# A two-layer decode kernel: some V tiles as the moving operand, and a new order of its instructions

## The chip, the core and the metric

The kernel runs on one core of one Trainium2 chip. Its time is the device time of that core in microseconds. Five engines work side by side and meet through semaphores: PE (TensorE, matmul; its weight loads are shown as PEld), DVE (VectorE), ACT (ScalarE), POOL (GpSimd) and SP (SyncE), which here only issues DMAs. 16 DMA engines carry all transfers of the core.

## The reference

One token for each of four batches goes through attention on a cache, a gated linear unit, and both again with the same weights:

```python
def _A_ref(x, k_cache, v_cache, wq, wo):          # x: 4 x 1 x 512
    q = (x @ wq).reshape(B, Sq, 32, 128).transpose(0, 2, 1, 3)
    k = jnp.repeat(k_cache, 4, axis=1)            # caches: 4 x 8 x 4096 x 128
    v = jnp.repeat(v_cache, 4, axis=1)
    p = _softmax(jnp.einsum("bhqd,bhkd->bhqk", q, k) * 128 ** -0.5)
    o = jnp.einsum("bhqk,bhkd->bhqd", p, v)
    return o.transpose(0, 2, 1, 3).reshape(B, Sq, 4096) @ wo
def _B_ref(x, w_gate, w_up, w_down):              # 512 -> 1792 -> 512
    h = _sigmoid(x @ w_gate) * (x @ w_up)
    return h @ w_down
x = A_x
x = x + _A_ref(_layernorm(x), A_k_cache, A_v_cache, A_wq, A_wo)
x = x + _B_ref(_layernorm(x), B_w_gate, B_w_up, B_w_down)
x = x + _A_ref(_layernorm(x), A_k_cache, A_v_cache, A_wq, A_wo)
x = x + _B_ref(_layernorm(x), B_w_gate, B_w_up, B_w_down)
```

Everything is bf16. One batch's K is 8 groups x 4096 x 128, 8 MiB, and so is its V; each group serves four query heads.

## The kernel before

**The data.** K and V come as half tiles of 512 KiB (128 partitions x 2048 elements), 16 for the K of a batch and 16 for its V, into a ring of 22 slots in SBUF. Weights have buffers of their own: wq and wo in four pieces of 1 MiB, wg, wu and wd of 1.75 MiB. K of a batch is used by both layers: most of its half tiles stay in their slots from the first layer's scores to the second layer's; the list `again` (L389) names those that are given up and loaded again instead (0, 3, 3 and 1 for the four batches). V is loaded once for each layer.

**The load order.** The string `order` (L388) is the order of all loads in SP's queue: `k` two K half tiles, `V` one group's V for the first layer (two half tiles), `v` one group's V for the second layer, `r` a batch's reloads, digits and other letters the weights. Each load waits for the last reader of its slot, and SP works in order, so a load that waits holds those behind it.

**The work of one batch b.** `attend` (L779) does scores and softmax for 16 heads (`s` = 0 or 1): DVE transposes the K half tiles in place (L537), PE multiplies (`scores`, L540, result S_ps, 16 rows in each of four strips of 32 partitions), DVE finds the maximum (L567 to L586), ACT takes the exponent (L591), PE and ACT turn the probabilities over (PT_ps, L596 to L610) into `pt_sb`. POOL and PE form the denominators. `values` (L635) multiplies with V: V is the stationary operand, 16 matmuls of 4 columns for each half tile, summed in O_ps; DVE scales (L653). `y_proj` (L657) multiplies with wo into Y_ps. `cross` (L698) then does the residual, the norm, gate and up (`glu`, L670), tanh (for the sigmoid), down (L685), residual and norm. `q_proj` (L496) makes the second layer's queries of that batch, `q_spread` (L511) lays them out (perm matmuls, then qbd), and the second layer's attention runs on the K that is still in the ring. Second-layer V work of batch b - 1 is placed between (`use_later`, L827). The last GLU is done for all four batches at once (`last_cross`, L715).

**What sets the order.** The code states operations with an engine, an estimated duration, a priority and the tiles read and written (`_Sched.put`, L46). `place` (L85) plays them through: each engine takes, of the operations that are ready, the one of best priority, SP goes in order, and a load gets the slot that is free first. The result is a fixed instruction order on every engine and a fixed slot for every load; `emit` (L187) writes it out with semaphores. Durations in the code steer that order and nothing else. Dependencies are by key: who writes a key waits for its readers.

Of the kernel before, what the change touches and what calls it, by code (L numbers as in the profile page):

```python
# [15 lines left out]
RAMP = 0.3  # L16

# [20 lines left out]
class _Sched:  # L38
# [7 lines left out]
    def put(self, eng, fns, dur, prio, reads=(), writes=(), dma=None, tiles=(), uses=(), nbytes=0, rate=RATE):  # L46
        op = _Op()
        op.eng, op.dur, op.prio, op.bytes, op.rate = eng, dur, prio, nbytes, rate
        op.fns = list(fns) if isinstance(fns, (list, tuple)) else [fns]
        op.sem, op.inc, op.needed = dma or eng, 16 if dma else 1, dma is not None  # L50
# [34 lines left out]
    def place(self):  # L85
# [17 lines left out]
        ramp = 0  # L103

# [17 lines left out]
        while True:  # L122
# [47 lines left out]
            else:  # L170
                pending[o.eng].remove(o)
                free_at[o.eng] = t + o.dur
# [30 lines left out]
def bass_interleave_layers__gqa_block_cached__glu_gated_glu__decode_kernel(nc, A_x, A_k, A_v, A_wq, A_wo, B_x, B_wg, B_wu, B_wd, out):  # L203
# [18 lines left out]
    NQB = 4  # L222
# [21 lines left out]
    x16 = sb("x16", [P, P], bf)  # L244
# [5 lines left out]
    gs = sb("gs", [P, NF * B])  # L250
    us_sb = sb("us_sb", [P, NF * B])
    hT = sb("hT", [P, NF * B], bf)
# [15 lines left out]
    p_sb = sb("p_sb", [P, 8, P], bf)  # L268
    pt1 = p_sb[:].rearrange("p c x -> p (c x)")[:, 0:512].rearrange("p (c g a h) -> p c g a h", c=8, g=4, a=4)
    NPT = 5  # L270
    pt_sb = [sb(f"pt_sb{i}", [P, 4, 8, 4, R], bf) for i in range(NPT)]
    oT1 = sb("oT1", [P, H], bf)
    oT2 = sb("oT2", [P, H, B], bf)
# [4 lines left out]
    negb = sb("negb", [P, P], bf)  # L278
# [3 lines left out]
    mt = sb("mt", [P, 32])  # L282
# [5 lines left out]
    sel_den = sb("sel_den", [P, 16])  # L288

# [4 lines left out]
    G_ps = ps("G_ps", [P, 512])  # L294
# [17 lines left out]
    S.put("sp", lambda e: e.dma_start(x16[0:16, :], A_x.rearrange("b o (k p) -> (b o k) p", k=KD)), 0.55, 0, writes=["x16"], dma="x")  # L312
# [8 lines left out]
    for key, ap, v in (("negb", negb[:], -1.0 / D), ("mhalf", mhalf, -0.5), ("xT", xT[:], 1.0)):  # L321
        S.put("dve", lambda e, ap=ap, v=v: e.memset(ap, v), 0.08, 0, writes=[key])
# [8 lines left out]
    for name, t, v in (("ml0", ml, 1.0), ("mt", mt, 0.0), ("S0", S_ps[0], 0.0), ("S1", S_ps[1], 0.0), ("S2", S_ps[2], 0.0)):  # L331
        S.put("dve", lambda e, t=t, v=v: e.memset(t[:], v), 0.4, 0, writes=[name])
# [5 lines left out]
    again = ((), ((6, 1), (7, 0), (7, 1)), ((5, 1), (6, 1), (7, 1)), ((7, 1),))  # L338
# [49 lines left out]
    order = '1k0kkkk23VkkVVkVVbdgacVVVuwrvkkkkkkVvkkVVVVVVVvkvvvvkrvkkkkkvvVkVVVVVVVvkvvvvrkkkkkVvvkvkVVVVVVVvvvvvvvvrvvvvvv'  # L388
    again = ((), ((6, 1), (7, 0), (7, 1)), ((5, 1), (6, 1), (7, 1)), ((7, 1),))  # L389
# [27 lines left out]
    def stat(c, n, prio, reads):  # L417
# [7 lines left out]
        fns = [mm(G_ps[:, c:c + n], negb[:], hi, True, False), mm(G_ps[:, c:c + n], negb[:], lo, False, True)]  # L425
        S.put("pe", fns, 0.1, prio, reads=["xs_hi", "xs_lo", "negb"], writes=["G"])
# [11 lines left out]
    def first_norm(prio):  # L438
        S.put("dve", lambda e: e.tensor_reduce(xsum[:, 0:B], x0[:], AX.X, ALU.add), 0.2, prio, reads=["x0"], writes=["xsum0"])
        stat(0, B, prio, ["xsum0"])  # L440
        S.put("dve", lambda e: e.tensor_copy(nm[0], G_ps[:, 0:B]), 0.15, prio, reads=["G"], writes=["nm0"])
# [7 lines left out]
        stat(4, B, prio, ["xsum4"])  # L449
        power(float(DH), G_ps[:, 4:4 + B], "G", rs_q[0], "rs_q0", B, prio)  # L450

    def add_y(b, y, scal, skey, res, rkey, mi, prio):
# [12 lines left out]
            "act", lambda e: e.activation(  # L465
                xw[:, 0, :], xj[:, b, :], ACTF.Square, bias=nm[mi][:, b:b + 1], accum_out=xsum[:, 1:2]
            ), 0.4, prio, reads=["xj", f"nm{mi}"], writes=["xw", "xsum4"],
        )

    def norm(b, mi, mult, rs, rs_key, prio):  # L470

        stat(0, 2, prio, ["xsum0", "xsum4"])
        new, old = nm[1 - mi][:, b:b + 1], nm[mi][:, b:b + 1]
        S.put("dve", lambda e: e.tensor_copy(new, G_ps[:, 0:1]), 0.15, prio, reads=["G"], writes=[f"nm{1 - mi}"])
# [6 lines left out]
                out=dd[:, 1:2], in0=dd[:, 0:1], scalar=dd[:, 0:1], in1=G_ps[:, 1:2], op0=ALU.mult, op1=ALU.add,  # L481
            ), 0.17, prio, reads=["dd", "G"], writes=["dd"],
# [79 lines left out]
    def softmax(u, rs, rs_key, prio):  # L562
# [69 lines left out]
        )  # L632
        return pi

    def values(l, b, s, pi, prio, gis=range(4)):  # L635
        if not len(gis):
            return
        for gi in gis:
# [263 lines left out]
```

## Time and profile before

| what | value |
|---|---|
| time, median of 8 runs | 336.48 us (334.58 to 340.37) |
| profiled execution: time / span | 338.83 us / 337.0 us |
| mean granted PE clock | 0.678 |
| PE busy | 204.5 us (61%), 5184 matmuls |
| DVE busy | 154.3 us (46%) |
| ACT busy | 60.6 us (18%) |
| POOL busy | 27.1 us (8%) |
| SP loads of K, V half tiles | 71, 128 |
| queue of all loads (q1) | 118.24 MB, its packets took 91.8% of 16 engines' span |

The span is from the first to the last instruction of one profiled execution; the time of that execution has a little more around it. The page also draws the span in 40 equal slices. Here are those of PE and DVE in tenths busy, and the PE clock that was granted, in tenths of full speed:

```profile
PE   0244543254486478666756686748627777696885
DVE  4592641002378862054889520417986501224213
PEclk9999999999997555555755555555757555557555
```

No engine is full over the span. The costliest groups of instructions (line, engine, operation, output<-inputs, count, busy us, mean ns of one, idle before them and what ended it):

```profile
L537 DVE STREAM_TRANSPOSE ring<-ring 128x1024 int32<-128x1024 int32 x71 | 85.9, 1228 | 22.7 <-DMA ring<-in_A_k_cache_dram 22.3
L644 PE MATMUL O_ps<-pt_sb,ring 128*128 128x4 bf16 x2048 | 67.2, 166 | 44.6 <-DMA ring<-in_A_v_cache_dram 30.5
L550 PE MATMUL S_ps<-ring,qbd 128*16 128x512 bf16 x512 | 56.6, 587 | 11.4 <-DVE ring L537 9.1
```

Matmuls overlap, so the mean of one is longer than the distance from one to the next.

### The profile page before, as it was taken

Reading aid. Unit: us, or ns where it says so; the run is one execution under the profiler, and the core shown is the slowest. Engines: PE = TensorE matmul, PEld = TensorE weight load, DVE = VectorE, ACT = ScalarE, POOL = GpSimd, SP = SyncE. Lnnn points to the kernel's source line nnn. Section 1 sums busy time; section 2 is a strip of 40 time slices with the busy share of each in tenths; the row PEclk is TensorE's granted clock in tenths of the full one; section 3 lists DMA queues with packets and bytes.
Section 4 is the critical chain, followed back from the end, with each engine's and each line's share of the span. In section 5 each row is a group of like instructions: output and inputs, shape, how many; then the busy total and the mean of one; then the engine's idle time right before and its main releaser. Section 6 shows DMA issues by size and latency. Waiting matters only on the chain.

```text
span 337.0 us, 11572 instructions
## 1 busy us (share of the span) xinstructions
PE 204.5 (61%) x5184; PEld 149.4 (44%) x5184; DVE 154.3 (46%) x390; ACT 60.6 (18%) x152; POOL 27.1 (8%) x106
## 2 busy tenths in 40 slices
PE   0244543254486478666756686748627777696885
PEld 0213222254443238666323466645214467663774
DVE  4592641002378862054889520417986501224213
ACT  1103103000006413000063130000524120002400
POOL 5101001000001101000011110000111010001101
PEclk9999999999997555555755555555757555557555
DMA  6999999999729999999999999988999999879930
GB/s 215 405 399 404 408 391 379 369 406 372 281 65 372 413 410 406 408 407 344 387 369 410 409 407 408 409 322 246 390 411 408 409 372 415 313 255 386 391 146 2
DMA packets 37906, 118.98 MB, mean 353 GB/s; under 512 B 3425, under 2 KB 9313, under 8 KB 37857
## 3 DMA queue, kind: packets, MB, share of 16 engines
q1 hardware_dynamic: 37824, 118.24, 91.8%
q8 instruction: 40, 0.66, 0.8%
q14 instruction: 10, 0.07, 0.1%
q10 hardware_dynamic: 32, 0.00, 0.0%
HBM read 118.23 MB, written 0.00 MB: 351 GB/s over the span
## 4 chain that ended last, share of the span: by engine, by line
DMA 40%; PE 25%; SPq 16%; issue 12%; DVE 5%; ACT 1%; POOLq 0%; POOL 0%; DVEq 0%; ACTq 0%
DMA ring<-in_A_v_cache_dram 25%; DMA ring<-in_A_k_cache_dram 9%; SPq L344 9%; PE O_ps L644 7%; SPq L365 7%; DMA wd<-in_B_w_down_dram 6%; PE S_ps L550 6%; PE Y_ps L304 6%; PE M_ps L304 4%; DVE ring L537 2%; PE G_ps L304 1%; DVE ml L567 1%; PE PT_ps L304 1%; ACT p_sb L591 1%; POOLq L864 0%
## 5 line engine op out<-in xcount | busy, mean ns | idle before, releaser
L537 DVE STREAM_TRANSPOSE ring<-ring 128x1024 int32<-128x1024 int32 x71 | 85.9, 1228 | 22.7 <-DMA ring<-in_A_k_cache_dram 22.3
L644 PE MATMUL O_ps<-pt_sb,ring 128*128 128x4 bf16 x2048 | 67.2, 166 | 44.6 <-DMA ring<-in_A_v_cache_dram 30.5
L644 PEld LDWEIGHTS O_ps<-pt_sb,ring 128*128 128x128 bf16 x2048 | 61.0, 104 | 57.9 <-DMA ring<-in_A_v_cache_dram 36.1
L550 PE MATMUL S_ps<-ring,qbd 128*16 128x512 bf16 x512 | 56.6, 587 | 11.4 <-DVE ring L537 9.1
L591 ACT ACTIVATE p_sb<-S_ps,cols 128x512 bf16<-128x512 f32 x32 | 24.6, 773 | 83.7 <-DVE cols L586 53.4
L653 DVE TENSOR_TENSOR oT<-O_ps,winv 128x12 bf16<-128x12 f32 (+3 forms) x29 | 5.0, 171 | 70.9 <-PE O_ps L644 70.7
L567 DVE TENSOR_REDUCE ml<-S_ps 128x1 f32<-128x512 f32 x32 | 21.5, 673 | 19.8 <-PE S_ps L550 19.8
L304 PE MATMUL Y_ps<-oT,wo 128*128 128x1 bf16 (+1 forms) x640 | 20.5, 166 | 12.8 <-DMA wo<-in_A_wo_dram 7.7
L550 PEld LDWEIGHTS S_ps<-ring,qbd 128*16 128x16 bf16 x512 | 12.9, 108 | 32.9 <-issue 18.5
L304 PEld LDWEIGHTS Y_ps<-oT,wo 128*128 128x128 bf16 x640 | 18.8, 104 | 15.0 <-DMA wo<-in_A_wo_dram 7.8
L304 PE MATMUL PT_ps<-ident_b,p_sb 128*128 128x64 bf16 x128 | 11.3, 230 | 19.3 <-ACT p_sb L591 19.3
L304 PEld LDWEIGHTS PT_ps<-ident_b,p_sb 128*128 128x128 bf16 x128 | 7.2, 116 | 26.4 <-ACT p_sb L591 21.9
L304 PE MATMUL M_ps<-xT,wq 128*128 128x1 bf16 (+1 forms) x512 | 15.4, 165 | 5.2 <-issue 3.7
L304 PEld LDWEIGHTS M_ps<-xT,wq 128*128 128x128 bf16 x512 | 14.6, 104 | 5.7 <-issue 4.0
L615 POOL TENSOR_TENSOR cols<-cols 128x1 f32<-128x1 f32 x16 | 3.1, 193 | 170.1 <-ACT p_sb L591 170.1
L434 POOL TENSOR_TENSOR cols<-cols 128x1 f32<-128x1 f32 (+1 forms) x10 | 6.6, 656 | 123.7 <-DVE cols L430 86.3
L526 ACT ACTIVATE qbd<-M_ps,mask_a 128x64 bf16<-128x64 f32 x32 | 10.0, 313 | 29.2 <-PE M_ps L304 28.5
L465 ACT ACTIVATE xw<-xj,cols 128x4 f32<-128x4 f32 x8 | 2.4, 298 | 70.6 <-DVE xj L460 70.6
L304 PE MATMUL Y_ps<-hT,wd 128*128 128x1 bf16 (+1 forms) x280 | 8.5, 166 | 10.2 <-issue 5.1
L599 ACT ACTIVATE p_sb<-PT_ps 128x512 bf16<-128x512 f32 x16 | 9.6, 597 | 21.7 <-PE PT_ps L304 17.2
L610 ACT ACTIVATE pt_sb<-PT_ps 128x512 bf16<-128x512 f32 x16 | 9.5, 596 | 19.4 <-PE PT_ps L304 19.3
L304 PEld LDWEIGHTS Y_ps<-hT,wd 128*128 128x128 bf16 x280 | 8.0, 104 | 10.6 <-issue 8.9
(103 smaller groups left out, 152.2 us busy)
## 6 DMA issues: line engine op xcount, KB each, us to landing
ring<-in_A_v_cache_dram SPq DMA_DIRECT2D x128, 512.0 KB, 9.6
ring<-in_A_k_cache_dram SPq DMA_DIRECT2D x71, 512.0 KB, 9.6
wq<-in_A_wq_dram SPq DMA_DIRECT2D x4, 1024.0 KB, 14.1
wo<-in_A_wo_dram SPq DMA_DIRECT2D x4, 1024.0 KB, 14.1
wg<-in_B_w_gate_dram SPq DMA_DIRECT2D x1, 1792.0 KB, 13.9
wu<-in_B_w_up_dram SPq DMA_DIRECT2D x1, 1792.0 KB, 16.0
wd<-in_B_w_down_dram SPq DMA_DIRECT2D x1, 1792.0 KB, 20.6
x<-in_A_x_dram SPq DMA_DIRECT2D x1, 4.0 KB, 1.6
```

The lines of the kernel that those rows point to most:

```text
L304: return lambda e: e.matmul(o, lhsT=l, rhs=r, start=start, stop=stop)
L344: return e.dma_start(ring[t.slot], t.src.rearrange("(p t) d -> p (t d)", p=P)[:, q * TS:(q + 1) * TS])
L365: S.put("sp", lambda e: e.dma_start(o, i), 0.43, 0, writes=[key], dma=key, nbytes=nbytes, rate=rate)
L434: "pool", lambda e: e.tensor_tensor(rs, vpe[:, 0:nb], mhalf[:, 0:nb], ALU.pow), 0.6, prio,
L526: "act", lambda e, a=a: e.activation(qbd[u % NQB][:].rearrange("p g n x -> p (g n) x")[:, :, 4 * a:4 * a + 4], M_ps[:, 256:320].rearrange( ...
L537: return e.transpose(v, v)
L550: return e.matmul(bank[32 * gi:32 * gi + 16, :], lhsT=qbd[u % NQB][:, gi, nn, :], rhs=kt[:, :, nn // 2, :, nn % 2], start=nn == 0, stop=nn ...
L567: "dve", lambda e, q=q: e.tensor_reduce(ml[:, q:q + 1], S_ps[banks[q]][:], AX.X, ALU.max, negate=True), 0.65,
L591: "act", lambda e, q=q: e.activation(p_sb[:, 4 * q:4 * q + 4, :].rearrange("p c x -> p (c x)"), S_ps[banks[q]][:], ACTF.Exp, bias=nbias, s ...
L599: "act", lambda e: e.activation(pt1.rearrange("p c g a h -> p (c g a h)"), PT_ps[:], ACTF.Copy), 0.65, prio,
L610: "act", lambda e: e.activation(pt_sb[pi][:].rearrange("p q c g h -> p (q c g h)"), PT_ps[:], ACTF.Copy), 0.65,
L644: return e.matmul(O_ps[:, gi * R:(gi + 1) * R], lhsT=ring[tile.slot][:, (t % HT) * DH:(t % HT + 1) * DH], rhs=pt_sb[pi][:, t % 4, t // 4, ...
```

## The change

- **Wide V.** Second-layer V of batch b - 1 that is used around `cross(b)` for b = 1, 2, 3 (36 half tiles, `NARROW[3]` is empty) goes through the new function `wide`: the probabilities are stationary (8 columns: two key blocks of four heads), V is moving with 256 columns, and the 8 matmuls of a half tile go round four strips of the new bank W_ps. Two groups share the bank's two halves. Then ACT copies W_ps to `w_hi` (bf16), DVE takes the rest into `w_lo`, and four small matmuls a group with the 0/1 matrix `sel_o` sum strips and halves into O_ps. All other V stays as it was.
- **Banks and buffers.** G_ps is gone; gate goes to M_ps, the norms' sums to M_ps or PT_ps. Some buffers are laid over others to make room: gs, us and hT in the second half of p_sb (and they share its key), x16 in w_hi, oT2 on q1T, mt on ml, negb as one column. qbd has 3 buffers, not 4. `pt_sb` has another layout.
- **Small operations.** The sum of squares in `add_y` is on DVE instead of ACT. Gate and up are planned piece by piece, so that they may alternate, and the norm may start after the second of four gate pieces. V and wo of the first layer alternate by group.
- **The planner.** PE durations come from a count of instructions (0.0268 a pair and 0.13 at the end), and at each 256th PE instruction the planner adds a wait if less than 5.7 has passed since the last such point. The priorities, `order` and `again` are new: reloads are 1, 3, 2 and 4 half tiles. The second query spread of the next batch is stated after the first half's attention.

The core of the diff:

```diff
+BLOCK = 256
+FETCH = 5.7
+PAIR = 0.0268
+DRAIN = 0.13
...
+                if o.eng == "pe":
+                    n = 2 * len(o.fns)
+                    to = BLOCK - begun % BLOCK
+                    if n >= to:
+                        at = t + o.dur * to / n
+                        wait = max(0.0, crossed + FETCH - at)
+                        o.dur += wait
+                        crossed = at + wait
+                    begun += n
+                free_at[o.eng] = t + o.dur - (DRAIN if o.eng == "pe" else 0.0)
...
-    NQB = 4
+    NQB = 3
+    WIDE = 0.43
+    NARROW = ((0, 1, 2, 3), (0, 1, 2, 3), (0, 1, 2, 3), (), (0, 1, 2, 3))
...
-    order = '1k0kkkk23VkkVVkVVbdgacVVVuwrvkkkkkkVvkkVVVVVVVvkvvvvkrvkkkkkvvVkVVVVVVVvkvvvvrkkkkkVvvkvkVVVVVVVvvvvvvvvrvvvvvv'
-    again = ((), ((6, 1), (7, 0), (7, 1)), ((5, 1), (6, 1), (7, 1)), ((7, 1),))
+    order = 'k10bkkkkk3Vk2VVkdVVcVagVVuwrvkkkkkkVvkkVVVVVVVvvkvvvkrkkkkvkvvVkVVVVVVVvvkvvvrkkkvvkvkkkVVVVVVVVrvvvvvvvvvvvvvv'
+    again = (((3, 1),), ((6, 1), (7, 0), (7, 1)), ((6, 1), (7, 1)), ((6, 0), (6, 1), (7, 0), (7, 1)))
...
-    PS0, PS1, PL0, PL1, PV0, PV1, PK0, PK1, PDEN, PEV = (1.24, 0.52, 0.5, 1, 1.15, 0.9, 2.1, 2.1, 0.72, 1.8)
+    PS0, PS1, PL0, PL1, PV0, PV1, PK0, PK1, PDEN, PEV = (1.77, 1.93, -0.4, 1.55, 2.05, 1.65, 2.13, 2.82, 2.29, 1.1)
...
+    def wide(l, b, s, pi, prio, gis):
+        n = len(gis)
+        for i, gi in enumerate(gis):
+            for q in range(2):
+                tile = V[l, b, 4 * s + gi, q]
+                fns = []
+                for j in range(HT // 2):
+                    def fn(e, i=i, gi=gi, q=q, j=j, tile=tile):
+                        a, t = j % 4, q * HT + 2 * j
+                        return e.matmul(
+                            W_ps[32 * a:32 * a + 2 * R, i * 256:i * 256 + 256],
+                            lhsT=pt_sb[pi][:, t // 4, gi, t % 4:t % 4 + 2, :].rearrange("p t h -> p (t h)"),
+                            rhs=ring[tile.slot][:, 2 * j * DH:(2 * j + 2) * DH],
+                            start=q == 0 and j < 4, stop=q == 1 and j >= 4,
+                        )
+                    fns.append(fn)
+                S.put("pe", fns, WIDE + DRAIN, prio, reads=[f"pt{pi}"], writes=["W"], tiles=[tile])
+        w = 256 * n
+        S.put(
+            "act", lambda e: e.activation(w_hi[:, 0:w], W_ps[:, 0:w], ACTF.Copy), 0.62 if n > 1 else 0.4, PEV, reads=["W"],
+            writes=["w_hi"],
+        )
+        S.put(
+            "dve", lambda e: e.tensor_tensor(w_lo[:, 0:w], W_ps[:, 0:w], w_hi[:, 0:w], ALU.subtract),
+            0.65 if n > 1 else 0.4, PEV, reads=["W", "w_hi"], writes=["w_lo"],
+        )
+        fns = []
+        for i, gi in enumerate(gis):
+            for x, half in enumerate((w_hi, w_lo)):
+                for t in range(2):
+                    fns.append(mm(
+                        O_ps[:, gi * R:(gi + 1) * R], half[:, i * 256 + t * DH:i * 256 + (t + 1) * DH],
+                        sel_o[:, t * R:(t + 1) * R], x == 0 and t == 0, x == 1 and t == 1,
+                    ))
+        S.put("pe", fns, 0, prio, reads=["w_hi", "w_lo", "sel_o"], writes=["O"])
...
-        for w, key, dst, bkey in ((wg, "wg", G_ps, "G"), (wu, "wu", Y_ps, "Y")):
+        for w, key, dst, bkey in ((wg, "wg", M_ps, "M"), (wu, "wu", Y_ps, "Y")):
...
-                S.put("pe", fns, 0.033 * len(fns), prio, reads=[xtkey, key], writes=[bkey])
-            if w is wg:
-                between()
+                S.put("pe", fns, 0, prio, reads=[xtkey, key], writes=[bkey])
+                if w is wg and f1 == 6:
+                    between()
...
-            ), 0.2, prio, reads=["gs", "us"], writes=["hT"],
+            ), 0.2, prio, reads=["p_sb1", "p_sb1"], writes=["p_sb1"],
...
-            "act", lambda e: e.activation(
-                xw[:, 0, :], xj[:, b, :], ACTF.Square, bias=nm[mi][:, b:b + 1], accum_out=xsum[:, 1:2]
-            ), 0.4, prio, reads=["xj", f"nm{mi}"], writes=["xw", "xsum4"],
+            "dve", lambda e: e.scalar_tensor_tensor(
+                out=xw[:, 0, :], in0=xj[:, b, :], scalar=nm[mi][:, b:b + 1], in1=xj[:, b, :], op0=ALU.add, op1=ALU.mult,
+                accum_out=xsum[:, 1:2],
+            ), 0.3, prio, reads=["xj", f"nm{mi}"], writes=["xw", "xsum4"],
```

## The prediction

> **What bounds the kernel now.** I read the page's 40 slices first, then the busy times in windows of 4 us, then the waits of SP's DMA queue and the PE timeline at the four places where the DMA falls off.
>
> ```profile
> GB/s 215 405 399 404 408 391 379 369 406 372 281 65 372 413 410 406 408 407 344 387 369 410 409 407 408 409 322 246 390 411 408 409 372 415 313 255 386 391 146 2
> DMA packets 37906, 118.98 MB, mean 353 GB/s; under 512 B 3425, under 2 KB 9313, under 8 KB 37857
> q8 instruction: 40, 0.66, 0.8%
> ```
>
> Most slices run at 404 to 415 GB/s: the kernel streams. At 409 GB/s its 118.98 MB take 290.9 us; the other 46 us of the 337.0 us span are holes. The windows date them (columns: window, busy time and count by engine, PE clock, DMA share, GB/s):
>
> ```profile
> 88.00:92.00 4.00, 0.80 (x26) 0.66 (x22) 1.86 (x6) 0.00 (x0) 0.00 (x0) 1.00 0.52 205
> 92.00:96.00 4.00, 2.34 (x72) 2.08 (x76) 3.96 (x7) 0.00 (x0) 0.56 (x1) 1.00 0.01 4
> 96.00:100.00 4.00, 4.00 (x48) 1.27 (x44) 1.77 (x6) 0.00 (x0) 0.00 (x0) 1.00 0.28 78
> ...
> 224.00:228.00 4.00, 1.15 (x44) 1.09 (x42) 0.83 (x5) 0.00 (x0) 0.55 (x1) 0.50 0.50 190
> 228.00:232.00 4.00, 3.28 (x124) 3.22 (x121) 2.70 (x3) 0.00 (x0) 0.00 (x0) 0.50 0.80 264
> ...
> 296.00:300.00 4.00, 3.82 (x142) 3.75 (x143) 1.05 (x5) 0.00 (x0) 0.55 (x1) 0.50 0.59 172
> ```
>
> A window loses 4 x (1 - GB/s / 409). Summed over neighbouring windows: start (0 to 12) 4.1 us; after batch 0 (88 to 108) 10.5; batch 1 (156 to 176) 2.6; batch 2 (220 to 240) 5.6; batch 3 (288 to 312) 5.7; end (320 to 337) 13.75; 3.5 scattered, mostly under the weights. 290.9 + 45.75 = 336.7, so the book closes.
>
> The four middle holes are one thing: 13 to 16 of the 22 ring slots hold K of a batch until its second-layer scores, which wait for the chain residual, GLU, down, q projection. SP then has no free slot:
>
> ```profile
> SPq L344 <- PE O_ps L644: 79.5, 50, 5.5
> ```
>
> (waiter, releaser: total us, times, longest). What makes the chain long shows in the PE timeline of batch 2 (start, us, line, operation, count, idle before):
>
> ```profile
> 215.09 0.69 PE L304 MATMUL Y_ps<-xT,wu 128*128 128x1 bf16 x20 [2.20 <-issue]
> ...
> 221.28 0.96 PE L304 MATMUL Y_ps<-hT,wd 128*128 128x1 bf16 x30 [2.46 <-issue]
> ...
> 227.73 1.02 PE L644 MATMUL O_ps<-pt_sb,ring 128*128 128x4 bf16 x33 [2.85 <-issue]
> ...
> 232.21 1.89 PE L550 MATMUL S_ps<-ring,qbd 128*16 128x512 bf16 x16
> ```
>
> PE waits for nothing recorded, and between these starts lie 128 and 127 load-and-matmul pairs and 6.2 to 6.45 us, though a pair issues in 27 ns where nothing holds it (32 V pairs in 0.85 us in the chain of waits). So here PE is limited by the arrival of instructions.
>
> **What the Trainium skill says.** "Runtime: NRT & Kernel Launch", section Instruction fetch mechanics: instructions come in 16 KiB blocks of 256 by the engine's own DMA queue, and the cost is mostly hidden. The trace agrees on the block (0.66 MB in 40 packets; gaps every 128 pairs) and not on the hiding: the gaps from 211 to 232 sum to 8.2 us. "TensorEngine Tiling (Array Packing)", section When to Use Tiling, advises swapping stationary and moving with column tiling for a small moving side, which is this edit. "TensorE: Matmul & The Clock Gate", section Measured speedup vs the span model, gives 2.38x for three column tiles. Here the S row agrees: one matmul lasts 587 ns, sixteen over four strips take 1.89 us, 118 ns each, at clock 0.50.
>
> **The change, part by part.**
>
> *Wide V.* 36 half tiles (12 in each of batches 1 to 3) take 8 matmuls of 256 columns instead of 16 of 4 columns, plus 72 matmuls with sel_o: PE goes from 5184 to 4968 pairs. No row shows the new matmul; half the S spacing gives 118 / 2 = 59 ns, 0.47 us a tile, against 0.43 to 0.59 for a narrow tile. PE time is even; what falls is the instruction count. I bound a tile by 0.43 and by 2.35 us (8 x 587 / 2, no overlap), and take 0.5.
>
> *Chain length.* Pairs from the first wg matmul to the first second-layer S: 448, 448, 432 before (batches 1, 2, 3), and 296, 304, 312 after by the changed instruction order. Of the drop 64 each is the second q projection, now behind the first 32 S matmuls. Before, these stretches took 142.63 to 160.41 (17.8 us), 211.15 to 232.21 (21.1) and 283.58 to 299.92 (16.3): 39.7, 47.0 and 37.8 ns a pair. So they lose 152 x 39.7 = 6.0, 144 x 47.0 = 6.8 and 120 x 37.8 = 4.5 us. Against that stands the wide matmul where PE and not the fetch binds (48, 56, 64 of them at 59 - 27 ns: 1.5 to 2.0 us), and the scores lose their cover: perm, qbd on DVE (93.50 to 93.89, after 92.75) and S now follow each other, about 1 us. Net 3, 4 and 1 to 2 us if PE binds throughout, the full figures if the fetch does.
>
> *What the holes become.* From the landing of the last first-layer V, 16 to 17 half tiles of 1.28 us (0.524 MB at 409 GB/s) can be loaded before a K slot must come free: the free slots, and one more for each filler tile used. That is 20.5 to 21.8 us, less some 2 from issue to data. Before, batch 2 took from 209.0 (its last V pairs) to 234.1 (end of its first S), 25.1; less 5 to 6 this just fits. I take batch 1 from 2.6 to 0.3 (-2.3), batch 2 from 5.6 to 0.7 (-4.9). Batch 3 also gets four reloads at the front of its queue instead of one behind eight v tiles, three tiles more to load without a free K slot: 5.7 to 0.5 (-5.2).
>
> *Batch 0* has no V filler. It waits for wd (landed 84.7) in both orders, which have the same bytes ahead of it. Then S precedes the second q projection (93.94 to 95.8), so the first four slots free 1.9 us earlier, and one reload fills 1.3 us of the hole: -3.2. A transpose that stands ahead of xT on DVE (1.23 us, waiting for that reload) may take 0.7 back; the fetch gap of 2.44 us at 88.13 would cover it. I leave it to the range (-1 to -4).
>
> *More bytes.* Reloads go from 7 to 10 half tiles: +1.57 MB, +3.85 us of DMA, partly in the holes counted above (so both are booked).
>
> *End.* Gate, up and down outputs share one key with p_sb's second half, so the up side now waits for tanh: in the last GLU two DVE operations (0.21 us each, with a gap) fall behind it, +0.45; its statistics come after 68 pairs instead of 56, +0.3. Sum +0.7. In cross the same wait is 0.23 us under two wide tiles; without that cover, 0.7 over three chains.
>
> *At nothing:* squares moved from ACT to DVE (0.30 + 0.19 there, 0.21 + 0.08 here, under the wg matmuls); PSUM banks renamed; the strided PT output; constants in one column; 5 POOL operations and one 0.49 us memset at the start, under the first loads; nine ACT copies and nine DVE subtractions (0.6 and 0.67 by the 128x512 rows L599 and L567), 11 us over a kernel in which ACT is busy 18% and DVE 46%. Where one stands ahead of xT or qbd, all of the chain waits.
>
> *Sum:* +3.85 - 3.2 - 2.3 - 4.9 - 5.2 + 0.7 = -11.05 us. I keep 1.5 back: in batch 1 a K transpose that waits for a load stands ahead of qbd on DVE, and after batch 3 PE's own path to the last Y took 44 us before (283.6 to 327.5), so about 39 now, against 41 of DMA (32 half tiles): there a lost us shows. -9.5: the profiled span goes from 337.0 to 327.5, its time from 338.83 to 329.3; on the median 336.48 the forecast is **327.0 us**.
>
> **The rivals.**
>
> *A, the chain shortens only by the PE-bound figures (3, 4, 1.5 us).* The fetch hides elsewhere, batch 2 keeps 2 us of hole, batch 3 leaves PE late at the end by 2.5. For it: batch 1's fetch gaps are only 0.74, 2.08 and 0.70. 327.0 + 4.5 = 331.5.
>
> *B, slower: the copy back becomes the wait.* One W bank serves all pairs of groups: until ACT (0.6), DVE (0.67) and three handovers of some 0.15 are done, 1.7 us, no further wide tile can run, and sel_o stands in PE's order ahead of the q projection. Two such rounds lie before S. If DVE is late by a transpose each time (1.23), the chain is longer than before: +6 against -5.5 and about 1 us of lost cover, 1.5 us at each of three batches. No hole closes and the bytes stay: 336.5 + 3.85 - 3.2 + 0.7 + 4.5 = 342.3. It decides from about 5 us of PE waits on w_lo or W in a chain. Against it: down (1.5 us) and other PE work stand between. The strips failing to overlap is the extreme of it (8 tiles x 1.8 us a chain, beyond 355); the S row speaks against.
>
> *C, nothing gained:* the new load order makes holes elsewhere (slots are fixed in advance; one late K transpose holds SP's whole queue) as large as those closed, 336. The page's even 404 to 415 between the holes says there is room.
>
> **How the numbers follow.** Main case 0.60 (own range 322 to 330.5), A 0.17, C 0.11, B 0.12. About 1% (3.4 us) is what a measurement tells from no change. Faster by over 1% (below 333.1): main and most of A, 0.77. Slower by over 1% (above 339.8): 0.12. Between: 0.11. The range 321 to 336 leaves out B, part of C and a small part below: 0.19.
>
> **What would show it.** Right: windows of batches 1 to 3 at 400 GB/s or more throughout; about 74 K loads; W rows of 16 pairs in about 1 us; PE issue gaps below 1.5 us between wg and S; batch 0's hole ending near 97.4 instead of 99.2. Wrong: PE or PEld waiting for DVE w_lo; W matmuls spaced over 100 ns; SP waiting for DVE transposes for many us; the same 2.5 us gaps; or DMA ending well before 312 with PE working on alone for over 14 us.

## Result and profile after

The changed kernel takes 335.15 us in the median (332.72 to 338.78, 18 runs) against 337.51 us before (333.93 to 340.65, 53 runs): ratio 0.9937, 95% interval [0.991, 0.9964]. Medians are of all runs; the ratios leave out runs over 1.5% above the fastest of their kernel. Two later comparisons of the same kernel gave 0.9863 [0.9813, 0.9914] and 0.9876 [0.9819, 0.9934]. So it is faster by 0.6 to 1.4%, 2 to 4.6 us, where 9.5 us were forecast. The profiled execution took 333.4 us with a span of 331.6 us, 5.4 us below the span of before.

The page of after: the slices that answer to those of before, the packets, and the new row of the groups.

```profile
GB/s 218 386 408 402 402 388 387 385 407 372 389 123 361 413 410 394 403 407 364 297 390 412 408 409 408 408 388 238 396 410 408 411 407 407 407 338 407 410 160 3
DMA packets 38337, 120.54 MB, mean 364 GB/s; under 512 B 3472, under 2 KB 9360, under 8 KB 38288
...
L673 PE MATMUL W_ps<-ring,pt_sb 128*8 128x256 bf16 x288 | 18.3, 386 | 7.7 <-DMA ring<-in_A_v_cache_dram 7.7
```

The dips are in the same places, and much shallower after batch 0 (12th slice) and batch 3 (36th) only. Windows of after (columns as before):

```profile
88.00:92.00 4.00, 0.94 (x23) 0.77 (x23) 1.25 (x7) 0.00 (x0) 0.40 (x1) 1.00 0.79 313
92.00:96.00 4.00, 2.82 (x28) 0.94 (x32) 4.00 (x6) 0.00 (x0) 0.16 (x1) 1.00 0.01 2
96.00:100.00 4.00, 2.84 (x76) 1.97 (x68) 3.59 (x11) 0.86 (x3) 0.00 (x0) 1.00 0.87 266
...
224.00:228.00 4.00, 3.48 (x44) 1.23 (x40) 3.16 (x7) 0.60 (x1) 0.55 (x1) 0.50 0.69 212
228.00:232.00 4.00, 3.49 (x104) 2.47 (x96) 3.79 (x11) 0.71 (x2) 0.00 (x0) 0.93 0.82 271
...
296.00:300.00 4.00, 3.88 (x114) 2.61 (x107) 2.45 (x10) 1.01 (x3) 0.00 (x0) 0.93 0.92 314
```

The book of the prediction (bytes at 409 GB/s and what each stretch of windows loses), worked out for the profiles of before, of after and of the most telling experiments. A hole is time in which the DMA runs below that rate. The stretches are a little wider than the prediction's, so a few tenths differ from its figures; the table leaves out some 7 us lost before 84 us, alike in all runs, and what lies between the stretches:

| us | before | after, 3 profiles | wide undone (e4) | fillers later (e8) | three moves (e10) | up twice (e15) |
|---|---|---|---|---|---|---|
| bytes at 409 GB/s | 290.9 | 294.7 | 294.7 | 294.7 | 294.7 | 294.7 |
| hole, batch 0 (84 to 108) | 10.5 | 7.2, 6.9, 7.1 | 7.0 | 6.6 | 6.5 | 6.1 |
| batch 1 (136 to 176) | 2.7 | 3.5, 2.2, 4.3 | 3.5 | 10.2 | 1.8 | 5.9 |
| batch 2 (204 to 244) | 5.5 | 4.1, 3.3, 4.2 | 4.5 | 9.5 | 3.4 | 6.1 |
| batch 3 (272 to 312) | 6.2 | 1.5, 1.7, 1.0 | 4.4 | 1.6 | 1.3 | 1.8 |
| end (from 312) | 14.1 | 13.3, 13.8, 13.9 | 13.9 | 13.4 | 13.9 | 14.5 |
| span | 337.0 | 331.6, 330.2, 333.3 | 336.1 | 343.1 | 329.4 | 337.3 |

Three profiles of one kernel differ by 3 us in span, nearly all of it in batches 1 and 2: that is how far one profile can be trusted. But in all three those two holes are open, where the prediction had closed them.

The chain from the GLU to the scores became shorter. From the first wg matmul to the first S of the second layer it takes 15.32, 15.27 and 13.34 us in batches 1, 2, 3, against 17.8, 21.1 and 16.3. What stands in it in batch 2 of after, on PE:

```profile
213.47 1.45 PE L673 MATMUL W_ps<-ring,pt_sb 128*8 128x256 bf16 x24
217.60 1.65 PE L326 MATMUL Y_ps<-p_sb,wd 128*128 128x1 bf16 x56 [2.67 <-DVE p_sb L754]
...
223.00 0.38 PE L326 MATMUL M_ps<-xT,wq 128*128 128x1 bf16 x8 [1.43 <-issue]
```

and on DVE at that time:

```profile
214.71 1.25 DVE L564 STREAM_TRANSPOSE ring<-ring 128x1024 int32<-128x1024 int32 x1 [2.37 <-DMA ring<-in_A_k_cache_dram]
...
215.98 1.24 DVE L564 STREAM_TRANSPOSE ring<-ring 128x1024 int32<-128x1024 int32 x1
...
217.37 0.17 DVE L754 SCALAR_TENSOR_TENSOR p_sb<-p_sb 128x14 bf16<-128x14 f32 x1
```

Fillers are the second-layer V tiles of the batch before, whose use in this stretch frees slots; here they are the wide tiles. They run as priced (24 matmuls in 1.45 us, 60 ns each). Then PE waits 2.67 us for hT (L754), because two K transposes of the next batch stand ahead of it on DVE and the first waits for its load. "DVE: scalar operands, raw-bit mode, write accounting and state across instructions", section Flops that outlive an instruction, in the Trainium skill, says that DVE has one in-order queue; the trace agrees: the gate, up and hT operations stand still behind the 2.37 us wait.

### The profile page after: what moved, and what is told of

It is laid out like the page before. It is cut to its first block, busy times and chain, and to the rows that moved or that the text cites. A ratio compares the mean times of both kernels' runs of the same rounds, so it can differ in the third digit from the quotient of the medians.

```text
span 331.6 us, 11181 instructions
## 1 busy us (share of the span) xinstructions
PE 208.0 (63%) x4968; PEld 143.0 (43%) x4968; DVE 164.8 (50%) x418; ACT 62.4 (19%) x145; POOL 27.9 (8%) x111
## 4 chain that ended last, share of the span: by engine, by line
DMA 51%; PE 19%; SPq 11%; issue 9%; DVE 8%; ACT 2%; POOLq 0%; POOL 0%; ACTq 0%; DVEq 0%
DMA ring<-in_A_v_cache_dram 29%; DMA ring<-in_A_k_cache_dram 22%; SPq L369 9%; PE S_ps L577 7%; PE M_ps L326 3%; DVE ring L564 3%; PE Y_ps L326 3%; PE W_ps L673 3%; PE O_ps L711 2%; SPq L390 2%; DVE ml L594 1%; ACT p_sb L618 1%; PE PT_ps L326 1%; DVE tr L611 0%; DVE tr L601 0%
## 5 line engine op out<-in xcount | busy, mean ns | idle before, releaser
L564 DVE STREAM_TRANSPOSE ring<-ring 128x1024 int32<-128x1024 int32 x74 | 89.9, 1230 | 27.2 <-DMA ring<-in_A_k_cache_dram 26.2
L711 PE MATMUL O_ps<-pt_sb,ring 128*128 128x4 bf16 x1472 | 50.8, 167 | 33.1 <-DMA ring<-in_A_v_cache_dram 29.9
L711 PEld LDWEIGHTS O_ps<-pt_sb,ring 128*128 128x128 bf16 x1472 | 45.3, 104 | 44.1 <-DMA ring<-in_A_v_cache_dram 30.5
L720 DVE TENSOR_TENSOR oT<-O_ps,winv 128x8 bf16<-128x8 f32 (+2 forms) x16 | 2.6, 166 | 58.5 <-PE O_ps L711 58.4
L594 DVE TENSOR_REDUCE ml<-S_ps 128x1 f32<-128x512 f32 x32 | 21.4, 668 | 13.8 <-PE S_ps L577 13.7
L673 PE MATMUL W_ps<-ring,pt_sb 128*8 128x256 bf16 x288 | 18.3, 386 | 7.7 <-DMA ring<-in_A_v_cache_dram 7.7
L326 PE MATMUL Y_ps<-oT,wo 128*128 128x1 bf16 x512 | 17.3, 165 | 6.3 <-DVE oT L720 3.5
L326 PEld LDWEIGHTS Y_ps<-oT,wo 128*128 128x128 bf16 x512 | 15.6, 104 | 7.8 <-DVE oT L720 4.2
L326 PE MATMUL Y_ps<-p_sb,wd 128*128 128x1 bf16 (+1 forms) x280 | 8.4, 166 | 9.5 <-DVE p_sb L754 5.6
L774 ACT ACTIVATE p_sb<-p_sb,cols 128x14 f32<-128x14 f32 x4 | 1.2, 307 | 67.7 <-DVE p_sb L518 46.7
L326 PEld LDWEIGHTS Y_ps<-p_sb,wd 128*128 128x128 bf16 x280 | 7.9, 104 | 11.1 <-DVE p_sb L754 7.1
## 6 DMA issues: line engine op xcount, KB each, us to landing
ring<-in_A_v_cache_dram SPq DMA_DIRECT2D x128, 512.0 KB, 10.2
```

The source lines that it names most:

```text
L326: return lambda e: e.matmul(o, lhsT=l, rhs=r, start=start, stop=stop)
L564: return e.transpose(v, v)
L594: "dve", lambda e, q=q: e.tensor_reduce(ml[:, q:q + 1], S_ps[banks[q]][:], AX.X, ALU.max, negate=True), 0.65,
L673: return e.matmul(W_ps[32 * a:32 * a + 2 * R, i * 256:i * 256 + 256], lhsT=pt_sb[pi][:, t // 4, gi, t % 4:t % 4 + 2, :].rearrange("p t h - ...
L711: return e.matmul(O_ps[:, gi * R:(gi + 1) * R], lhsT=ring[tile.slot][:, (t % HT) * DH:(t % HT + 1) * DH], rhs=pt_sb[pi][:, t // 4, gi, t % ...
```

## Experiments

Where nothing else is said, a run is made from the changed kernel. In those that change an order, a few lines after the planner move operations in one engine's list; the other engines' orders, all slots and all loads stay. Their diffs give the order in words, not the code. Theories are numbered as in the expectations: 1 DVE's transposes, 2 instruction fetch, 3 the added bytes, 4 the wide form does nothing, 6 fillers used late, 7 fillers and scores both (there is no 5).

**The change again (e0).**

> The changed kernel again, unchanged, to have a second profile and its spread beside the runs below. Every theory: median 333.5 to 336.5, ratio to before 0.988 to 0.998. Theory 1 (K transposes that wait for a load stand ahead of chain operations in DVE's queue) expects the same two stalls again: DVE waits of 1 to 2.5 us for k_cache loads just before the second hidden product (down) in batches 1 and 2, and DMA holes of 3 to 4.5 us there. If the profiled stalls were accidents of one execution, at least one of them is gone here.

332.02 to 335.78, median 333.06, ratio 0.9863 [0.9813, 0.9914], both a little below what was expected. The stall in batch 2 is there again (2.59 us for p_sb), so it is no accident of one execution. That of batch 1 is gone ahead of down (0.73 us in the profile of after); 1.15 of 2.13 us ahead of S remained.

**Transposes later (e1).**

```diff
-DVE: ... K transpose, gate centre, K transpose, up centre, hT, ..., xs_lo, ...
+DVE: ... gate centre, up centre, hT, ..., xs_lo, K transpose, K transpose, ...
```

Transposes between q2T and qbd go behind qbd in the same way.

> Nine K transposes are moved behind the chain operations that they stood ahead of, in DVE's order alone; every other engine, slot and load is as in the changed kernel. Theory 1 (DVE's queue): in batch 1 the start of down comes 0.7 us earlier and that of the scores 2 us earlier, in batch 2 down comes 2.7 us earlier; the holes of batches 1 and 2 shrink from 3.5 and 4.2 to about 1 and 1.5 us, and the time falls by 3 to 5 us against the changed kernel: 330 to 332, ratio to before 0.978 to 0.986. Theory 2 (instruction fetch still sets the chain): PE issue gaps grow by what DVE gives back, time within 1 us of the changed kernel, ratio 0.99 to 0.997. Theory 3 (the three extra half tiles eat the gain): holes may shrink but later ones grow, time within 1 us.

335.84 us, ratio 0.9934 [0.991, 0.9958]: nothing gained. Theory 1 as the only cause falls. The PE timeline of this run, batch 1, its four waits with no recorded cause:

```profile
133.77 0.94 PE L733 MATMUL O_ps<-pt_sb,ring 128*128 128x4 bf16 x30 [1.14 <-issue]
...
139.97 0.59 PE L695 MATMUL W_ps<-ring,pt_sb 128*8 128x256 bf16 x6 [0.68 <-issue]
...
146.16 0.57 PE L348 MATMUL Y_ps<-xT,wu 128*128 128x1 bf16 x16 [1.63 <-issue]
...
152.22 1.23 PE L348 MATMUL M_ps<-xT,wq 128*128 128x1 bf16 x40 [1.41 <-issue]
```

They are 6.20, 6.19 and 6.06 us apart with 128 pairs between each two: the fetch of instructions, just behind the wall that was taken away. The trace's packet records confirm it: each of the four waits ends 2.44 to 2.50 us after a packet of 16 KB on the instruction queue (q8) started. In batch 2 it hides under a wrong name:

```profile
215.97 1.64 PE L348 MATMUL Y_ps<-p_sb,wd 128*128 128x1 bf16 x56 [1.90 <-DVE w_lo L709]
...
222.10 0.37 PE L348 MATMUL M_ps<-xT,wq 128*128 128x1 bf16 x8 [2.16 <-issue]
```

Down does not read w_lo, and its hT was done at 213.41. But from its start to the next gap are 128 pairs (56 + 8 + 8 + 56) and 6.13 us, so it stands at a block's edge; packets of the instruction queue started 2.43 us ahead of it and 2.42 us ahead of the next gap's end. It starts at 6.56 us after the first wg matmul, against 7.41 in e0. In batch 3 the moved transposes (3.49 us) came to stand ahead of the statistics' copy, which held PE for 2.39 us, and the hole there grew to 4.8: a fault of this experiment's place, not of the idea.

**Wide V undone (e4).** `NARROW = ((0, 1, 2, 3),) * 5`, planned again.

> The wide V alone is undone: all V tiles run as stationary operand, 16 matmuls of 4 columns; load order, reloads, bank layout and priorities are those of the changed kernel, and the planner places the order again. Theory 4 (the wide form contributes nothing; the new order and reloads made what gain there is): 334 to 336, ratio to before 0.99 to 0.998. The prediction's reason (fewer instructions in the chain, at 40 to 47 ns a pair): some 70 pairs more in each of three chains, 3 us each before what the holes leave, so 337 to 343, ratio 1.00 to 1.02, and PE issue gaps over 2 us again between gate and scores.

339.67 us, ratio 1.0048 [1.0026, 1.007], against 0.9863 for e0 beside it: theory 4 falls, without the wide form the new order is slower than before (priorities made for narrow tiles weren't tried). It costs 5.9 us of span. The chains of batches 1 and 2 are as long as with it (15.09 and 15.21 us), that of batch 3 is 2.5 us longer (15.97 against 13.44), and its hole 2.7 us larger. So 72 and 64 pairs more left two of the three chains as long as they were.

**Fewer reloads (e5, e9).** `again[0] = ()` and `again[3] = ((7, 1),)`; in e9 the latter only.

> The reload lists of before for batches 0 and 3 (none and one half tile, instead of one and four) in the changed kernel; bytes fall by four half tiles, 2.10 MB, 5.1 us at 409 GB/s. Theory 3 (the extra bytes eat the gain): 330 to 332, ratio 0.978 to 0.986, no hole larger. The prediction's reason (each reload fills a hole that would be there without it): the hole of batch 0 grows by 1.3 us and that of batch 3 by about 3.9 us, time 334 to 337, ratio 0.99 to 1.00.

> Only batch 3's reloads go back from four half tiles to one; bytes fall by 1.57 MB, 3.85 us at 409 GB/s. Theory 3 (these bytes eat the gain): the hole of batch 3 grows by at most 2 us, time 1.5 to 2.5 us below the changed kernel, ratio 0.98 to 0.985. The prediction's reason (they fill a hole that would be there without them): the hole of batch 3 grows by 3 to 4 us, time within 1 us, ratio 0.985 to 0.995.

e5: 333.54, ratio 0.9853 [0.9807, 0.99]; e9: 334.73, ratio 0.988 [0.9854, 0.9905]. Both are where the changed kernel is; by its ratio alone e5 would fit theory 3, and the holes decide. In e9 batch 3's hole grew from 1.5 to 4.8, nearly the 3.85 us saved; in e5 batch 0's grew to 8.5 and batch 3's to 3.8. A reload is worth the hole that it fills, as the prediction booked it; theory 3 falls.

**Fillers earlier, alone (e6) and with the transposes (e7).**

```diff
-PE: down, sel_o, W, q projection, statistics, W W W, perm, S
+PE: down, sel_o, W, W W W, q projection, statistics, perm, S
```

> In PE's order alone, three wide V tiles of batches 1 and 2 move from behind the second layer's q projection to ahead of it, behind the tile that already stands there; all else as in the changed kernel. Theory 6 (a hole opens because the filler tiles are used late: their slots come free only behind down and the q projection): three slots come free about 3.5 us earlier, the holes of batches 1 and 2 (2.2 to 3.5 and 3.3 to 4.2 us) shrink by 1.5 to 2.5 us each, time 1 to 4 us below the changed kernel, ratio to before 0.976 to 0.986. Theory 2 (the chain to the scores, paced by instruction fetch at 6.1 us for 128 pairs, sets the holes): S starts 0.7 to 1.5 us later in both batches and the holes grow by as much, time 1 to 3 us above, ratio 0.99 to 1.00.

> The later K transposes on DVE and the earlier wide tiles on PE together. If theory 6 is right and DVE's stalls matter only once the fetch does not cover them: at least as fast as the earlier tiles alone in batches 1 and 2; but batch 3 has the later transposes too, which came with a hole of 4.8 us instead of 1.5 there: 332 to 335 us, ratio 0.983 to 0.993. Theory 1 (DVE's queue is the only cause): at or below 331, ratio under 0.982.

e6: 332.45 us, ratio 0.9832 [0.9801, 0.9862], a little below the changed kernel's own three and within the interval of e0; e7: 334.78, 0.9881 [0.9841, 0.9922], with batch 3's hole at 4.1, near what was expected. What e6 shows is in SP's waits from 205 to 240 us (total, times, longest). First e0:

```profile
SPq L369 <- PE W_ps L673: 10.6, 5, 3.7
SPq L369 <- PE S_ps L577: 3.6, 2, 2.2
```

then e6:

```profile
SPq L377 <- PE W_ps L681: 8.0, 5, 3.3
SPq L377 <- PE S_ps L585: 7.5, 2, 5.4
```

SP waits less for the fillers and more for the scores: the wait moved, and the holes stayed (3.3 in batch 1, 3.5 in batch 2). The ratio is in the range of theory 6, but the holes, which it expected to shrink by 1.5 to 2.5 each, are not smaller: it falls as the only cause.

**Fillers later (e8).**

```diff
-PE: down, sel_o, W, q projection, statistics, W W W, perm, S
+PE: down, sel_o, q projection, statistics, perm, S, W, W W W
```

> The opposite move: the four wide tiles that stand between down and the first second-layer scores in batches 1 and 2 go behind those scores. 32 pairs leave the chain. Theory 6: four slots come free 5 to 9 us later, holes of both batches grow by 2 to 4 us each, time 4 to 8 us above the changed kernel, ratio 1.00 to 1.015. Theory 2: the chain to S is shorter by 32 pairs, 1.5 us at 47 ns each, holes shrink by as much, time 2 to 3 us below, ratio 0.978 to 0.986.

346.36 us, ratio 1.0231 [1.0199, 1.0263], more than expected. The chains are 1.1 and 1.4 us shorter than in e0 (13.92 and 14.06 us), and the holes are 10.2 and 9.5. SP's queue in batch 2:

```profile
214.26 8.18 SPq L380 DMA_DIRECT2D ring<-in_A_v_cache_dram  x6
234.66 4.18 SPq L380 DMA_DIRECT2D ring<-in_A_k_cache_dram  x8
```

No load is issued between 222.44 and 234.66. This decides against a theory by chain length alone: here it counts more when the fillers are used than when S starts.

**Three moves together (e10), with own keys (e11), with one filler (e12), and the change beside them (e13).** e10 is e6 with the transposes later in batches 0 to 2, and those ahead of xT in batches 0 and 3 behind the statistics. e11 adds, in the waits:

```diff
-up centre waits for tanh (shared key p_sb1)
+hT waits for tanh
```

> Three moves together, orders only: the K transposes later in batches 0 to 2 (not in batch 3, where they made a stall of their own), the transpose that stands ahead of the residual's xT in batches 0 and 3 behind the first statistics, and the three wide tiles of batches 1 and 2 ahead of the q projection. Theory 7 (a hole is a shortage of free slots that ends when BOTH the fillers are used and the scores free K; one alone moves the wait to the other): holes of batches 0 to 3 about 5.7, 2.0, 3.3 and 1.0 instead of 6.9, 2.2 to 3.5, 3.3 to 4.1 and 1.6, span 327 to 329, ratio to before 0.975 to 0.983. If the fetch alone sets them: holes as in the changed kernel, ratio 0.985 to 0.995.

> The same three moves, and the up side of the GLU no longer waits for the tanh of the gate side (their product does): the shared key is undone in the waits, orders unchanged. The prediction priced the shared key at 0.45 us in the last GLU and 0.2 to 0.7 over the three chains. Expected: the end (from 312 us on) 0.4 us shorter than in the run with the three moves alone, the time 0.4 to 0.8 us lower, ratio lower by 0.001 to 0.002; a rival: nothing, since the fetch of the next block of instructions covers the wait.

> As the run with own keys, but only the first of the three wide tiles moves ahead of the q projection. With all three, the profile shows PE waiting 0.2 to 1.1 us for the last fillers' loads ahead of the q projection. Theory 7: one tile gives the free slot without that wait: S in batch 2 starts 1 us earlier, holes within 0.5 us of the run with three, time the same or up to 1 us lower, ratio 0.973 to 0.982. If slots freed early are worth more than the chain: 1 us higher.

> The changed kernel once more, beside the three runs above on one chip, since its two comparisons so far gave 0.9937 and 0.9863. Every theory: 333 to 336 us, ratio 0.985 to 0.995, above the three runs beside it if theory 7 holds.

e10: 331.25, ratio 0.9792 [0.9743, 0.984]; e11: 331.74, 0.9792 [0.9741, 0.9843]; e12: 332.3, 0.9838 [0.9779, 0.9896]; e13: 334.27, 0.9876 [0.9819, 0.9934]. e10 and e11 have the lowest ratios of all kernels here; their intervals and e13's just overlap. Holes of e10 are 6.5, 1.8, 3.4 and 1.3, near what theory 7 expected. In batch 1 both moves together do what neither does alone: the hole is 1.5 to 2.0 in e7, e10, e11 and e12, against 3.4 with the transposes alone (e1), 3.3 with the fillers alone (e6) and 2.2 to 4.3 in the changed kernel. In batch 2 they do nothing: 3.3 to 4.7 against 3.3 to 4.2. The own keys shorten the last GLU, from its first gate operation on DVE to the start of hT, by 0.34 us (2.35 to 2.01), which the median doesn't show. One filler gives 0.12 us of chain in batch 2 against e11, whose keys it has (0.35 against e10), not 1, and the hole of e10 (3.4; 4.7 in e11).

**Dose of the chain (e14, e15, e16).** 56 pairs taken out of gate and up, or put in, in batches 1 and 2. e14 and e15 are made from e10, e16 from the changed kernel. e14 and e16 leave out half of these products, so their output is not the reference's. The code, shortened:

```diff
+if o.glu and o.glu[0] in (1, 2):
+    o.fns = [f for i, f in enumerate(o.fns) if i % 4 in (0, 3)]   # e14, e16
+    o.fns = o.fns + o.fns                                          # e15, wu only
```

> The kernel with the three moves (later transposes, earlier wide tiles), and in batches 1 and 2 half of the gate and up products is left out (k of 0 and 3 of four): 56 pairs less between xT and down, orders and slots unchanged. Theory 7 with the fetch as the chain's pace: everything behind the gate, fillers and scores alike, comes 56 x 47 ns = 2.6 us earlier, the holes of batches 1 and 2 (1.8 and 3.4) fall to 0.3 or less and about 1, time 3.5 to 4.5 us lower, ratio to before 0.966 to 0.970. If PE's own work is the pace (27 ns a pair): 1.5 us earlier each, holes 0.5 and 2, time 2.5 to 3 us lower, ratio 0.970 to 0.974. If the chain doesn't set these holes: no change, ratio 0.977 to 0.982.

> The opposite dose on the same kernel: the up product of batches 1 and 2 is done twice (the second overwrites the first), 56 pairs more between xT and down. Fetch as the pace: 2.6 us later each, holes of batches 1 and 2 about 4.4 and 6.0, time 5 us higher, ratio 0.992 to 0.997. PE as the pace: 1.5 us later, time 3 us higher, ratio 0.986 to 0.991. If the chain doesn't set the holes: no change.

> The same half of gate and up left out, in the changed kernel itself (transposes and wide tiles where the change puts them). There K transposes that wait for loads hold hT on DVE, and the loads land when they land: theory 7 with DVE's queue as the second wall expects that down in batch 2 hardly moves (0 to 1 us), holes of batches 1 and 2 fall by 0.5 to 1.5 in all, time 0.5 to 2 us below the changed kernel, ratio 0.98 to 0.986. If DVE's queue is no wall: 3 to 5 us below, ratio 0.972 to 0.979.

e14: 330.68 us, ratio 0.981 [0.9745, 0.9874], no better than e10. e15: 338.12 us, 1.0016 [0.9991, 1.0041], some 2% above e10. e16: 332.06 us, 0.9868 [0.9782, 0.9954], no different from the change; e14 and e16 have four runs each. So in the time a longer chain costs a lot, and 56 pairs less gain nothing that shows. 56 pairs more made it 3.3 and 2.0 us longer (59 and 36 ns a pair; so the price doesn't tell fetch from PE) and the holes 4.1 and 2.7 us larger. 56 pairs less started down 2.5 us earlier in batch 2 of e14, counted from the first wg matmul, and S only 0.6. PE of e14 shows the next wall:

```profile
211.98 1.65 PE L358 MATMUL Y_ps<-p_sb,wd 128*128 128x1 bf16 x56
...
216.13 0.60 PE L705 MATMUL W_ps<-ring,pt_sb 128*8 128x256 bf16 x8 [0.67 <-DMA ring<-in_A_v_cache_dram]
217.41 0.60 PE L705 MATMUL W_ps<-ring,pt_sb 128*8 128x256 bf16 x8 [0.69 <-DMA ring<-in_A_v_cache_dram]
218.68 0.59 PE L705 MATMUL W_ps<-ring,pt_sb 128*8 128x256 bf16 x8 [0.67 <-DMA ring<-in_A_v_cache_dram]
219.21 1.86 PE L358 MATMUL M_ps<-xT,wq 128*128 128x1 bf16 x64
```

The fillers now come ahead of their own data: they follow each other at 1.27 us, the pace of their loads (0.524 MB at 409 GB/s take 1.28), and the q projection stands behind them. In e16, with the transposes where the change has them, down in batch 2 comes 7.36 us after the first wg matmul, in e0 7.41, for 56 pairs less: DVE's queue is a wall of its own, as expected. But behind down the chain is shorter in batch 2 of e16:

```profile
218.59 1.86 PE L327 MATMUL M_ps<-xT,wq 128*128 128x1 bf16 x64
...
222.61 3.31 PE L578 MATMUL S_ps<-ring,qbd 128*16 128x512 bf16 x32 [0.52 <-DVE qbd L548]
```

With fewer pairs ahead of it, the edge that stood in the q projection (1.53 us in e0, 1.43 in the profile of after) came to lie ahead of down, under PE's wait for hT. The fillers behind the q projection and S both come some 1.7 us earlier, S 13.71 us after the first wg matmul against 15.44 in e0, and the hole is 1.7 against 3.3 to 4.2. It is one profile, and the median of four runs doesn't show it.

## Why the prediction was wrong

- **What held.** Batch 0: -3.2 forecast, -3.3 in the profile; in part by luck, since wd, which was taken to land at the same time, landed 0.9 us earlier (83.8), and S started 2.6 us earlier, not 1.9. Batch 3: -5.2 forecast, -4.5 to -5.2. Bytes: +3.85, as counted. The wide tile: 0.5 us, as taken. The chain: 2.5, 5.8 and 3.0 us shorter, inside the bounds of 3 to 6, 4 to 6.8 and 1 to 4.5 but for half a us in batch 1. The share of the wide form in it, a price of 40 to 47 ns a pair, was argued, and e4 shows it in batch 3 alone. One reading was loose: 587 ns over 118 is 5.0, more than four strips side by side can give, so 587 ns, a mean of matmuls that overlap, is not the time of one alone. The wide tile's price came out all the same (60 ns a matmul, 59 taken).
- **The step that failed: "this just fits. I take batch 1 from 2.6 to 0.3 (-2.3), batch 2 from 5.6 to 0.7 (-4.9)."** Over the three profiles of after batch 1 went to 2.2 to 4.3 and batch 2 to 3.3 to 4.2: 3.2 and 3.4 us are missing at the middle one. With that the sum of -11.05 becomes -4.45, beside -5.4 in the profile. The count behind it was right: in e0 17, 16 and 17 half tiles are loaded from the landing of the last first-layer V until a K slot comes free. Two things failed in "this just fits". The first: it was not asked when the last of those slots come free. A PE line of e0, then SP's queue (start of first, us until the end of last, loads; the last line from 225 us on):

```profile
206.82 0.58 PE L711 MATMUL O_ps<-pt_sb,ring 128*128 128x4 bf16 x16 [0.21 <-DMA ring<-in_A_v_cache_dram]
...
200.29 2.43 SPq L369 DMA_DIRECT2D ring<-in_A_v_cache_dram  x4
203.61 1.59 SPq L369 DMA_DIRECT2D ring<-in_A_k_cache_dram  x2
206.21 8.52 SPq L369 DMA_DIRECT2D ring<-in_A_v_cache_dram  x6
218.56 6.08 SPq L369 DMA_DIRECT2D ring<-in_A_k_cache_dram  x4
...
226.09 1.97 SPq L369 DMA_DIRECT2D ring<-in_A_k_cache_dram  x4
```

 The last V is there at 206.8, and twelve loads of 1.28 us bring the DMA to 222.2. The thirteenth is issued at 218.56, behind the wide tile that follows down; the next three at 222.63 and after, behind the three wide tiles that follow the q projection. There the windows of e0 run dry:

```profile
221.00:222.00 1.00, 0.37 (x14) 0.36 (x15) 0.00 (x0) 0.00 (x0) 0.00 (x0) 0.50 0.79 315
222.00:223.00 1.00, 1.00 (x23) 0.65 (x24) 0.80 (x5) 0.00 (x0) 0.04 (x1) 0.50 0.40 164
223.00:224.00 1.00, 0.65 (x15) 0.18 (x4) 0.34 (x2) 0.43 (x1) 0.51 (x1) 0.50 0.49 127
```

 The second: the sum has no slack. Sixteen loads of 1.28 us less the 2 us that the prediction took from issue to data (an estimate) cover 18.5 us, seventeen 19.8; the 25.1 of before less 5 to 6 are 19.1 to 20.1. In e0 the first load into a slot that S frees is issued 20.1, 19.3 and 16.7 us after that landing in batches 1, 2 and 3 (batch 2: 226.09 - 206.8). By the prediction's own measure only batch 3 fits, and only its hole closed. And once the DMA had run dry, it lost 1.5 us more on its way back (last section), which the sum has at nothing.

 Experiments move both ends. e8, the same tiles used later, made the same holes more than twice as large; e15, a longer chain to fillers and scores, made them 4.1 and 2.7 us larger than in e10. With all four fillers of batch 2 early (e10), the sixteen loads are out by 219.84, the DMA runs at 385 or more until 225, and the hole begins where S frees the first K slots (issue at 225.90, 19.6 us after the landing): no smaller than without the move. In e16, where fillers and S come earlier, that issue is 17.6 us after the landing and the hole 1.7. So in batch 2 both ends are tight, and to move one is not enough.
- **The reserve of 1.5 us** named the right suspect in batch 1 (a transpose ahead of qbd) and priced it at too little. In batch 2, where 2.67 us of it stand ahead of hT, it was not looked for. But e1 says that moving the transposes alone brings little, and e16 that 56 pairs less don't bring down forward while the transposes stand there: fetch, DVE's transposes and the fillers' landing are walls close behind each other.
- **Rivals.** A (331.5) was nearest in time and right in part: batch 2 kept a hole (2 us forecast, 3.3 to 4.2 measured), and the one fetch gap left in its chain, 1.43 us where they summed to 8.2, has a share in it (e16). Its late end of 2.5 didn't come (13.3 to 13.9 against 14.1). B fell; PE's wait for w_lo in e1 is the fetch (packet records above). C fell: outside the old holes the new order loses 1.2 us at most (108 to 136, and nothing from 176 to 204 and 244 to 272).
- **The end:** +0.7 forecast, 13.3 to 13.9 against 14.1, so nothing shows; the shared key alone costs 0.34 of it (e11).
- **The base.** The forecast stood on 336.48, the median of 8 runs; that of all 53 is 337.51. The profile of before (338.83 us) lies 1.3 above the median of its 53 runs, that of after 1.75 below its own. So the pair of profiles differs by 5.4 and the medians by 2.4.

Open: why batch 1 of the changed kernel gave holes from 2.2 to 4.3 in three profiles. They go with PE's wait for qbd ahead of S (1.15, 2.13 and 2.34 us for 2.2, 3.5 and 4.3), but in e1 that wait is 0.52 and the hole 3.4. Open is also how small batch 2's hole gets with both ends moved on purpose; in e16 it was where the block's edge fell. A second bank for W_ps, which would let fillers run between the fourth wide tile and down, wasn't tried.

## What to carry to other kernels

When a ring of buffers feeds a stream, write down for each of the next loads when its buffer comes free, and compare that time with the time at which the stream needs it; the number of buffers alone says nothing of the last ones. Work that is there to free buffers must not come late (e8 lost some 11 us by it), and ahead of its own data it gains nothing (e14). Walls that stand within a few us of each other do not add: price the removal of one by the distance to the next, and test them together.

## What the runs showed of the hardware

- **The fetch of instructions has a pace of its own.** Edges of PE's blocks, 128 pairs of weight load and matmul, are 6.06 to 6.20 us apart in batch 1 of e1, while loads run at 375 to 415 GB/s. "Runtime: NRT & Kernel Launch", section Instruction fetch mechanics, in the Trainium skill, calls the crossing mostly hidden; here it left waits of 0.68 to 2.16 us at the edges in batches 1 and 2 of e1, each ending 2.42 to 2.50 us after a packet of the instruction queue started. In a profile such a wait can bear the name of a semaphore that the waiting operation doesn't need (w_lo ahead of down, 1.90 us).
- **After a dry spell the DMA stays below its usual rate for some 8 us.** Windows of e10, in which SP issued ten loads from 225.90 to 231.12:

```profile
226.00:227.00 1.00, 1.00 (x16) 0.27 (x8) 1.00 (x2) 0.00 (x0) 0.00 (x0) 0.72 0.14 41
227.00:228.00 1.00, 1.00 (x40) 0.91 (x37) 1.00 (x2) 0.00 (x0) 0.00 (x0) 1.00 0.83 229
228.00:229.00 1.00, 1.00 (x47) 0.98 (x45) 0.88 (x4) 0.00 (x0) 0.00 (x0) 1.00 0.90 188
...
232.00:233.00 1.00, 1.00 (x16) 0.30 (x12) 1.00 (x2) 0.49 (x1) 0.47 (x3) 0.50 0.93 303
233.00:234.00 1.00, 1.00 (x28) 0.69 (x24) 1.00 (x2) 0.00 (x0) 0.00 (x0) 0.50 1.01 320
```

 The engines are busy (0.83 to 1.01) and move 188 to 320 GB/s where 409 is usual. From 228 to 235 us that costs 1.5 us, nearly half of the hole of 3.4: the way back costs about as much as the dry spell itself (1.8 from 225 to 228). After longer dry spells it is much the same: below 409 in nearly every window from 99 to 107 us in before and from 236 to 245 in e8. Its cause wasn't tried.
